# Twenty product units ahead of the chain, preparation without a floor, GpSimd for the first experts' split, and VectorE copies from step 13

## The chip, the cores and the metric

The kernel runs on one core of a Trainium2 chip. Its engines work in parallel and meet at semaphores: TensorE (PE in the rows) multiplies matrices, VectorE (DVE), ScalarE (ACT) and GpSimd (POOL) work element by element, and SyncE (SP), ScalarE and GpSimd issue DMAs. The metric is the time of one execution in device microseconds (us).

## The reference, cut to what matters

Three stages follow one another. The first is a delta rule over 768 time steps with a 48 x 48 state for each of 32 heads; the second routes each of 3072 rows to the best of eight experts; the third is a dense layer on the rows that come out.

```python
for t in range(S):                                   # _attn_ref
    kt, vt, bt = (k_n[:, :, t], v[:, :, t], beta[:, :, t, None])
    y[:, :, t] = np.einsum('bhd,bhde->bhe', q[:, :, t], state)
    v_old = np.einsum('bhde,bhd->bhe', state, kt)
    state = state + bt[:, :, :, None] * np.einsum('bhd,bhe->bhde', kt, vt - v_old)
...
e_idx = np.argmax(x @ w_gate, axis=1)                # _moe_ref: x is y, 3072 rows of 384
h = np.maximum(x[mask] @ w1[e], 0.0)                 # for each expert e
out[mask] = gate_w[mask, None] * eom[mask, e, None] * (h @ w2[e])
...
h = np.maximum(np.maximum(x @ w1, x @ w2), x @ w3)   # _moe2_ref
return h @ w_out
```

## The kernel before

The 768 time steps are cut into 24 chunks of 32. Within a chunk the recurrence is a triangular system, so the kernel inverts one 32 x 32 triangle for each chunk, batch and head, and then needs only matrix products from chunk to chunk. This second part is the **chain**: 24 steps, each of which needs the state that the step before it left.

**Product units.** `prods(p, j)` (L150 to L178) makes the products of keys with keys and keys with queries for the two chunks of pair p and one half j of the heads: 32 matmuls (64 rows in the profile) on TensorE, two copies on ScalarE, a mask on GpSimd (L147). There are 24 such units. After the second half of a pair ScalarE issues the store of the products (`gd`, from slice 2 on, L174) and the loads of the two `KQT` chunks (112 x 1024 values of 4 bytes, 448 KB each) that lie two pairs ahead. `NA` says how many units stand in front of the chain; the rest are put at 0.05, 0.50, 0.95, ... of the chain's steps.

**Inversion.** Four chunks make a slice, six slices in all. VectorE inverts a slice in 30 small steps (L239 and L245, both operands in on-chip memory). Before it comes the preparation: `inv_load` reads the stored products back (`Z<-gd`, SyncE), `inv_n1` takes the diagonal and the triangle on GpSimd (`vss`, L195; affine select, L196), `inv_n2` makes scales on ScalarE (`vn`, L202) and `inv_n3` finishes them on VectorE and GpSimd (L216 to L225, with the scaling of Z, L218). A planner in `run` spreads the inversion's steps over the chain by a budget of VectorE time in each step (`BUD`, `take`) and puts the four preparations `prep` = 2.8, 2.2, 1.5 and 0.6 steps ahead of the slice's start.

**A step of the chain.** `c_ks` multiplies by the state (`pR`, L318) and VectorE subtracts (`R`, L321); `c_u` multiplies by the inverted triangle (`pU`, L340), whose two halves go out in four copies each (`Ubd`, L348 on ScalarE or L350 on VectorE); `c_s` updates the state (`pS`, L360), again copied in two halves (`Sbd`, L367 or L369); `c_y` makes the output rows. Up to step `END` - 1 ScalarE makes all copies, from `END` on VectorE makes the second halves. SyncE loads the step's `kv` (L294) and inverted triangles (`TT`, L302), and GpSimd scales half of `kv` (`vscale`, L308), two steps ahead of the use. `R` of step i needs the scaled `kv` of step i.

**The experts' start.** From step 7 on routed rows are scattered into a table (`tab`, L474, GpSimd). From step 15 the weights of the first two experts are loaded (`r`, L679, SyncE) and split into a high and a low part (`w_0h` by a cast, L695; `w_0l` by a subtraction, L696): three pieces of 1024 columns from step 18.2, four of 768 from 19.3, three of 1024 from 23.0. The raw tile of the second group is the one into which the third group is loaded. At steps 21 to 23 the first rows are gathered (`xg`, L837) and turned (`pt`, L852). After the chain come ten runs of expert work and six blocks of the dense layer, TensorE-bound for the most part.

Program order sets each engine's order: the lists in `run` are written out engine by engine as they stand, and an engine takes its instructions strictly one after the other.

Of the kernel before, what the change touches and what calls it, by code (L numbers as in the profile page):

```python
# [22 lines left out]
def merge(*lists):  # L23

    items = []
    for li, l in enumerate(lists):
        n = len(l)
        for j, f in enumerate(l):
            items.append(((j + 0.5) / n, li, j, f))
    items.sort(key=lambda t: t[:3])  # L30
    return [t[3] for t in items]


class Attn:
# [9 lines left out]
    def __init__(s, ctx, tc, psum, big, hp, gp, kqt, knv, bt, wgt, xd, tab, ctab, cum, ident, wrm, x2):  # L44
        s.tc, s.nc, s.psum, s.big, s.hp, s.gp = tc, tc.nc, psum, big, hp, gp
        nc = tc.nc
        s.kqt, s.knv, s.btd, s.wgtd, s.xd, s.tab, s.ctab, s.cum = kqt, knv, bt, wgt, xd, tab, ctab, cum
        s.ident, s.wrm, s.ones, s.x2 = ident, wrm, wrm[:, 0:128], x2
        s.NI = 24
        s.NP = 12  # L50
        s.NSL = 6
        s.RLB = "m"
        s.XB, s.xTs, s.RLK = 1, {}, 0
        s.CUT = 0.95
        s.NL = 4
        s.NA = 14
        s.LATE = 0.4
        s.W = (0, 1, 0)
        s.END = 16
        s.TU, s.TB, s.MF = (22.92, 22.95, 22.97), "TRT", 2  # L60

        s.BUD = (5.0, 5.6, 4.6, 5.0)

        s.ORD = {0: 0, 1: 14, 2: 36, 3: 50, 4: 66, 5: 80}
        s.prep = (2.8, 2.2, 1.5, 0.6)
        cp = s.cp = ctx.enter_context(tc.tile_pool(name="acst", bufs=1))
        s.p2 = ctx.enter_context(tc.tile_pool(name="ap2", bufs=2))
        s.dr = ctx.enter_context(tc.tile_pool(name="adr", bufs=1, space=DRAM))
        nc.scalar.preload_act_table_set("natural_log_exp_and_others")
        s.chain = False  # L70
        s.RT, s.RD, s.LT = (15.4, (15.9, 0.3), (17.4, 0.35), (20.7, 0.25)), 0.5, ((18.2, 0.45), (19.3, 0.35), (23.0, 0.05))
        s.KQT, s.AT, s.Gd, s.kv, s.TT, s.x, s.inv = {}, {}, {}, {}, {}, {}, {}
# [415 lines left out]
    def run(s, pre, tail):  # L488
        nc, NI, NP = s.nc, s.NI, s.NP
        for i in range(s.NL):  # L490
            s.loadKQ(i)
        s.consts()
        s.warm(9)
        A = [lambda p=p, j=j: s.prods(p, j) for p in range(NP) for j in range(2)]
        for k in range(4):
            A[k]()
        s.inv_load(0)
        for f in (s.inv_n1, s.inv_n2, s.inv_n3):
            f(0)
        B = [u[2] for u in s.steps(s.ORD)[:30]]  # L500
        s1 = s.ORD[1]
        for f in merge(B[:s1 // 3], [A[4], A[5]]) + merge(B[s1 // 3:s1 // 2], [A[6], A[7]]):
            f()
        s.inv_load(1)
        for f in (s.inv_n1, s.inv_n2, s.inv_n3):
            f(1)
        for f in merge(B[s1 // 2:], [A[8], lambda: s.load32(0), A[9], s.empty, A[10], lambda: s.load32(1), A[11], lambda: s.inv_load(2), A[12], A[13]]):
            f()
        s.inv_end(0)
        s.warm(8, s.inv[0]["tt"])  # L510
        s.inv_store(0)
        s.vscale(0)
        s.vscale(1)

        spr = [[] for _ in range(NI + 1)]
        put = lambda t, f: spr[int(t + 1)].append(((t + 1) % 1, f))
        t, left = [-1.0], [s.BUD[0]]
        s.ends = []

        def take(c):  # L520
            while left[0] < c:
                t[0] = int(t[0]) + 1.0 if t[0] >= 0 else 0.0
                left[0] += s.bud(int(t[0]))
            left[0] -= c
            b = s.BUD[0] if t[0] < 0 else s.bud(int(t[0]))
            t[0] = (int(t[0]) if t[0] >= 0 else -1) + min(0.99, max(0, 1 - (left[0] + c) / b))
        for starts in (s.ORD,):
            for st, c, f, en in s.steps(starts)[30:]:
                take(c)
                put(t[0], f)  # L530
                for sl in st:
                    t0 = t[0]
                    for dt, g in zip(s.prep, (s.inv_load, s.inv_n1, s.inv_n2, s.inv_n3)):
                        if sl > 2:
                            put(max(0.6, t0 - dt), lambda g=g, sl=sl: g(sl))
                        elif sl == 2 and g != s.inv_load:
                            put(-1 + (t0 + 1) * (0.3, 0.5, 0.9)[(s.inv_n1, s.inv_n2, s.inv_n3).index(g)], lambda g=g: g(2))
                    s.ends.append(("start", sl, t0))
                for sl in en:
                    take(1.4)  # L540
                    put(t[0], lambda sl=sl: s.inv_end(sl))
                    assert t[0] + s.LATE < 4 * sl - 1, (sl, t[0])
                    put(t[0] + s.LATE, lambda sl=sl: s.inv_store(sl))
                    s.ends.append((sl, t[0]))
        for k, f in enumerate(A[s.NA:]):
            put(0.05 + k * 0.45, f)
        for t, f in pre(s):
            put(t, f)
        s.chain = True
        for i in range(-1, NI):  # L550
            sp = [f for _, f in sorted(spr[i + 1], key=lambda x: x[0])]
            if i < 0:
                for f in sp:
                    f()
                continue
            q, k = i // 4 - 1, i % 4
            x0 = [lambda: s.r_g(q)] if q >= 0 and k == 1 else [lambda: s.r_p(q)] if q >= 0 and k == 2 else []
            f1 = [lambda: (s.x_store(i - 1), s.r_t(i - 1))] if i else []
            f2 = [lambda: s.r_l(q)] if q >= 0 and k == 0 else []
            s.load32(i + 2)  # L560
            if i >= 7:
                s.r_s({19: [0, 1], 20: [2, 3], 21: [], 22: [], 23: [0, 1]}.get(i, [(i - 7) % 4]))
            n = round(len(sp) * s.CUT) if i < 20 else sum(t < s.CUT for t, _ in spr[i + 1])
            wm = lambda k: [lambda: s.warm(s.W[k])]
            fl = [lambda: s.c_ks(i), lambda: s.c_qs(i)] + x0 + wm(0) + merge([lambda: s.c_u(i)] + f1, sp[:n]) + wm(1)
            fl += [lambda: s.c_s(i)] + merge([lambda: s.c_y(i)] + f2, sp[n:]) + wm(2)
            fl += [lambda: s.loadT(i + 2), lambda: s.vscale(i + 2)]
            for f in fl:
                f()
        tail(s)  # L570


class Decode:
# [17 lines left out]
    def units(s, raw, w):  # L591

        nc, V, N = s.nc, s.nc.vector, s.N
        n, a = s.pieces.pop(0)
# [30 lines left out]
class Moe:  # L625
# [394 lines left out]

    def ahead(s, a):

        V = s.nc.vector
        v = {}

        def later(key, n, t, d):
            def go(j):
                if (key, n) not in v:
                    v[key, n] = s.split(key, n, V, V)
                v[key, n][j]()  # L1030
            return [(t + d * j, lambda j=j: go(j)) for j in range((3, 4)[n])]

        def lists():
            s.ids(0)
            s.ids(1)

        def rows(k):
            for c in range(2):
                s.gather(k, c)

        def turned():
            z = [a.p2.tile([128, 1024], F32R, tag="Z", name=f"xT0{j}", bufs=4) for j in range(2)]
            s.xT[0] = [tuple(z[c // 2][:, (c % 2 * 2 + j) * 256:(c % 2 * 2 + j) * 256 + 256] for j in range(2)) for c in range(3)]

        def turn(c):
            if c == 0:
                turned()
            s.xpose(0, c, a.TB[c])
        def raws(key, n, slot, t, d):
            us = s.raws(key, n, lambda: s.btile(slot, f"r{n}_{key}", F32), 3)  # L1050
            return [(t + d * j, u) for j, u in enumerate(us)]
        out = [(a.RT[0], s.first), (a.RT[0] + a.RD, s.first_values), (19.3, s.parts), (21.0, lists),
               (21.3, lambda: rows(0)), (21.6, lambda: rows(1))]
        for (key, n, slot), (t, d) in zip(((0, 0, 0), (0, 1, 1), (1, 0, 1)), a.RT[1:]):
            out += raws(key, n, slot, t, d)
        for (key, n), (t, d) in zip(((0, 0), (0, 1), (1, 0)), a.LT):
            out += later(key, n, t, d)
        out += [(t, lambda c=c: turn(c)) for c, t in enumerate(a.TU)]
        out += [(23.1 + 0.1 * f, lambda f=f: s.m1(0, f)) for f in range(a.MF)]
        return out  # L1060
# [201 lines left out]
```

## Time and profile before

| what | value |
|---|---|
| median of 3 runs | 861.08 us (859.71 to 863.37) |
| the profiled execution's own time | 862.21 us |
| span of its instructions | 860.5 us |
| TensorE busy | 745.3 us (87%) |
| VectorE busy | 487.8 us (57%) |
| ScalarE busy | 303.9 us (35%) |
| GpSimd busy | 247.8 us (29%) |

The table counts the whole execution. The change touches the first 340 us or so; there the engines' shares differ from those of the whole, which is why the rows below are taken stretch by stretch. A row of the timeline gives start, duration, engine, line, operation, what is written and read, the count of merged instructions, and in brackets the engine's idle time before and what ended it.

### The profile page before, as it was taken

How to read it: one execution, taken by the hardware profiler on the slowest of the kernel's cores; microseconds unless marked ns; L12 is line 12 of the kernel's file. 1: busy time of each engine (PE TensorE's matmuls, PEld its weight loads, DVE VectorE, ACT ScalarE, POOL GpSimd, SP SyncE). 2: the span in 40 equal slices, each digit the busy share in tenths (PEclk: the TensorE clock that was granted, in tenths of full speed). 3: DMA queues.
4: the chain of work that ended last, by engine and by line, in shares of the span. 5: the costliest groups of instructions: out<-in, count | busy, mean ns of one | idle time of the engine just before them, and what ended most of it. 6: DMA issues, size and time to landing. Idle time of an engine off the chain costs nothing.

```text
span 860.5 us, 20328 instructions
## 1 busy us (share of the span) xinstructions
PE 745.3 (87%) x8516; PEld 631.0 (73%) x8517; DVE 487.8 (57%) x1142; ACT 303.9 (35%) x693; POOL 247.8 (29%) x326
## 2 busy tenths in 40 slices
PE   7615777788677987999989999999999999999997
PEld 5504555455455886989888889889888898988886
DVE  3896668994575753788899997132231323223130
ACT  2203556777433332454444353122121222212121
POOL 5715446732333232166455322000001010100101
PEclk9997879999978998999999999999999999999999
DMA  8743755444926226667786783921002020000001
GB/s 225 172 133 100 182 117 151 110 122 128 251 55 171 74 60 189 217 214 230 260 259 227 242 301 131 384 82 48 26 1 74 1 73 2 19 19 1 37 1 40
DMA packets 85756, 110.28 MB, mean 128 GB/s; under 512 B 53860, under 2 KB 67115, under 8 KB 82971
## 3 DMA queue, kind: packets, MB, share of 16 engines
q1 hardware_dynamic: 57259, 87.08, 32.4%
q10 hardware_dynamic: 19360, 11.42, 5.5%
q0 software_dynamic: 9040, 10.42, 4.1%
q8 instruction: 69, 1.13, 0.6%
q14 instruction: 28, 0.23, 0.1%
HBM read 79.53 MB, written 29.36 MB: 127 GB/s over the span
## 4 chain that ended last, share of the span: by engine, by line
PE 45%; DVE 11%; DMA 7%; issue 3%; SPq 1%; ACT 1%; POOL 1%; POOLq 0%; DVEq 0%; ACTq 0%
PE pm L864 26%; PE pz L864 8%; PE po L864 6%; PE ph L864 3%; DMA wd<-work 3%; DMA wm<-wd 2%; DVE hl L889 1%; DVE work L609 1%; SPq L821 1%; DVE work L611 1%; DMA work<-in_ma_dram 1%; DVE work L607 1%; DVE work L608 1%; DVE work L612 1%; DMA TT<-td 1%
## 5 line engine op out<-in xcount | busy, mean ns | idle before, releaser
L864 PE MATMUL pm<-xhm,wm 128*128 128x512 f32 x648 | 204.8, 396 | 1.9 <-DMA wm<-wd 1.9
L937 DVE TENSOR_TENSOR work<-work,pm 128x512 f32<-128x512 f32 x72 | 49.5, 688 | 186.8 <-PE pm L864 186.8
L864 PEld LDWEIGHTS pm<-xhm,wm 128*128 128x128 f32 x648 | 121.8, 188 | 31.2 <-DMA wm<-wd 2.3
L864 PE MATMUL pm<-xlm,wm 128*128 128x512 f32 x324 | 128.2, 396 | 0.0
L950 POOL DMA_INDIRECT out_dram<-work,idm x24 | 23.7, 986 | 303.7 <-ACT work L949 289.2
L939 ACT CAST hmh<-work 128x512 fp32r<-128x512 f32 x36 | 22.4, 622 | 156.3 <-DVE work L937 156.3
L864 PE MATMUL pz<-wm,hmh 128*128 128x384 f32 x320 | 73.7, 334 | 0.0
L239 DVE TENSOR_TENSOR zt<-Z 128x30 f32<-128x30 f32 (+14 forms) x219 | 71.5, 365 | 3.2 <-POOL Z L218 2.6
L864 PEld LDWEIGHTS pm<-xlm,wm 128*128 128x128 f32 x324 | 61.0, 188 | 14.4
L348 ACT COPY Ubd<-pU 32x192 f32<-32x192 f32 x160 | 49.5, 309 | 52.6 <-PE pU L340 49.7
L245 DVE TENSOR_TENSOR Z<-Z,zt 128x30 f32<-128x30 f32 (+14 forms) x219 | 61.0, 318 | 0.0
L864 PEld LDWEIGHTS pz<-wm,hmh 128*128 128x128 f32 x320 | 57.2, 188 | 0.5
L360 PE MATMUL pS<-Ubd,kv 128*48 128x192 f32 x368 | 44.4, 377 | 14.7 <-ACT Ubd L348 10.9
L837 POOL DMA_INDIRECT xg<-xd,ids x32 | 44.6, 1393 | 41.4 <-PE pt L852 29.2
L164 PE MATMUL pg<-KQT 48*32 48x64 f32 x1536 | 38.1, 279 | 16.6 <-DMA KQT<-in_kqt_dram 9.8
L360 PEld LDWEIGHTS pS<-Ubd,kv 128*48 128x48 f32 x368 | 23.7, 138 | 38.7 <-ACT Ubd L348 20.6
L164 PEld LDWEIGHTS pg<-KQT 48*32 48x32 f32 x1536 | 32.5, 143 | 23.4 <-issue 15.9
L367 ACT COPY Sbd<-pS 48x384 f32<-48x384 f32 x78 | 36.8, 472 | 14.1 <-PE pS L360 12.9
L899 ACT COPY y<-po 128x256 f32<-128x256 f32 (+6 forms) x30 | 13.3, 444 | 78.4 <-PE po L864 78.4
L318 PE MATMUL pR<-Sbd,KQT 112*32 112x96 f32 x736 | 23.9, 256 | 18.1 <-ACT Sbd L367 13.8
L308 POOL TENSOR_TENSOR kv<-kv,TT 128x384 f32<-128x384 f32 x20 | 21.0, 1050 | 64.2 <-DMA TT<-td 32.4
L864 PE MATMUL pz<-wm,hml 128*128 128x384 f32 x112 | 37.4, 334 | 0.0
(303 smaller groups left out, 1648.9 us busy)
## 6 DMA issues: line engine op xcount, KB each, us to landing
raw<-in_w_dram SPq DMA_DIRECT2D x13, 1536.0 KB
kv<-in_knv_dram SPq DMA_DIRECT2D x24, 384.0 KB
wd<-work SPq DMA_DIRECT2D x24, 384.0 KB
wm<-wd SPq DMA_DIRECT2D x8, 1152.0 KB
KQT<-in_kqt_dram ACTq DMA_DIRECT2D x20, 448.0 KB
xd<-x SPq DMA_DIRECT2D x24, 192.0 KB
r<-in_w_dram SPq DMA_DIRECT2D x9, 512.0 KB
raw<-x SPq DMA_DIRECT2D x6, 768.0 KB
```

What stands on the lines that cost most here:

```text
L164: nc.tensor.matmul(ps[b * 32:b * 32 + 32, o:o + 64], kq[:, 0, :], kq.rearrange("p k t -> p (k t)"), start=True, stop=True, tile_position=( ...
L239: nc.vector.tensor_mul(t, Z[:, a:e, m].unsqueeze(2).to_broadcast([128, e - a, n]), Z[:, m, m + 1:].unsqueeze(1).to_broadcast([128, e - a, n]))
L245: nc.vector.tensor_add(Z[:, a:e, m + 1:], Z[:, a:e, m + 1:], t)
L318: nc.tensor.matmul(ps[b * 32:b * 32 + 32, g * 96:g * 96 + 96], s.KQT[i][:, b, g, 0, :], s.Sbd[0:112, b, g, :], start=True, stop=True, tile ...
L348: nc.scalar.copy(dst, src)
L360: nc.tensor.matmul(s.pS[q][j * 64:j * 64 + 48, g2 * 192:g2 * 192 + 192], s.kv[i][:, 0, h, :], s.Ubd[h // 4][:, h % 4, :], start=(i == 0 an ...
L367: nc.scalar.copy(dst, src)
L837: s.nc.gpsimd.indirect_dma_start(t[0:r.ct], None, s.xd[0:2049] if k < 2 else s.xd, bass.IndirectOffsetOnAxis(s.gid[k][0:r.ct, c, 0:1], 0))
L864: s.nc.tensor.matmul(ps, a, b, start=(start and k == 0), stop=(stop and k == n - 1))
L937: nc.vector.tensor_max(m, m, ps)
L939: nc.scalar.copy(hi, m)
L950: nc.gpsimd.indirect_dma_start(s.out, bass.IndirectOffsetOnAxis(i[:, c, 2:3], 0), y, None, bounds_check=3071, oob_is_err=False)
```

## The change

`NA` goes from 14 to 20: six more product units stand ahead of the chain, and the last four take the first places in it. The lower limit of 0.6 steps falls away for the preparation of slices 3 to 5. `END` goes from 16 to 13, so steps 13 to 15 have their second copies on VectorE. The split of the first two experts' weights is given to GpSimd, both the cast and the subtraction.

```diff
-        s.NA = 14
+        s.NA = 20
...
-        s.END = 16
+        s.END = 13
...
-        for f in merge(B[s1 // 2:], [A[8], lambda: s.load32(0), A[9], s.empty, A[10], lambda: s.load32(1), A[11], lambda: s.inv_load(2), A[12], A[13]]):
+        for f in merge(B[s1 // 2:], [A[8], lambda: s.load32(0), A[9], s.empty, A[10], lambda: s.load32(1), A[11], lambda: s.inv_load(2)] + A[12:s.NA]):
...
-                            put(max(0.6, t0 - dt), lambda g=g, sl=sl: g(sl))
+                            put(t0 - dt, lambda g=g, sl=sl: g(sl))
...
-        V = s.nc.vector
+        G = s.nc.gpsimd
...
-                    v[key, n] = s.split(key, n, V, V)
+                    v[key, n] = s.split(key, n, G, G)
```

On TensorE in step 2 of the chain, before: `pU` is that step's product, `pg` are product units (pair and half), `pX` turns the step's output rows, `pwarm` is a dummy product, `pS` the update of the state.

```order
L340 MATMUL pU0_2_1596<-R2_1565,T0_998 32x48 x16
L340 MATMUL pU1_2_1597<-R2_1565,T0_998 32x48 x16
L164 MATMUL pg9_1_1644<-KQT18_1209 32x64 x32
L391 MATMUL pX1_1698<-ident_80,x1_1506 128x128 x3
L164 MATMUL pg10_0_1705<-KQT18_1209 32x64 x16
L164 MATMUL pg10_0_1705<-KQT21_1436 32x64 x16
L485 LDWEIGHTS wrm_58
L485 MATMUL pwarm_1755<-wrm_58 128x512
L360 MATMUL pS0_160<-Ubd0_156,kv2_1061 48x192 x4
```

The same place now:

```order
L340 MATMUL pU0_2_1784<-R2_1753,T0_1229 32x48 x16
L340 MATMUL pU1_2_1785<-R2_1753,T0_1229 32x48 x16
L391 MATMUL pX1_1847<-ident_80,x1_1731 128x128 x3
L485 LDWEIGHTS wrm_58
L485 MATMUL pwarm_1866<-wrm_58 128x512
L360 MATMUL pS0_160<-Ubd0_156,kv2_1302 48x192 x4
```

No product unit stands between `pU` and `pS` of step 2 any more. From `R` of step 2 to `R` of step 5 there were five units and are none; from step 1 to step 2 there were two and is one; in step 0 there are three as before.

On SyncE ahead of the chain and in its first steps, before: `Z2` and `Z3` are the products of slices 2 and 3 read back, `kv` the chunks' keys and values.

```order
L294 DMA kv1_801<-in_knv_dram 128x768
L184 DMA Z2_867<-gd2_164 128x1024
L294 DMA kv2_1061<-in_knv_dram 128x768
L184 DMA Z3_1213<-gd3_165 128x1024
L294 DMA kv3_1303<-in_knv_dram 128x768
```

And now:

```order
L294 DMA kv1_771<-in_knv_dram 128x768
L184 DMA Z2_831<-gd2_164 128x1024
L184 DMA Z3_1253<-gd3_165 128x1024
L294 DMA kv2_1302<-in_knv_dram 128x768
L294 DMA kv3_1531<-in_knv_dram 128x768
```

The load of slice 3 has moved ahead of `kv2`. VectorE's order in these steps has not changed by a row; on GpSimd two masks that stood ahead of slice 3's `vss` now stand behind it, and six masks stand ahead of the first scaling of `kv`.

On GpSimd in steps 18 to 21, before: `kv` rows are the scaling, `tab` the scatter, `rohb` and `cum` the count of rows, `xg` the gather.

```order
L460 COPY rdat3_4290<-tok_194 128x4
L308 TENSOR_TENSOR kv20_4240<-kv20_4240,TT20_4380 128x384
L474 DMA tab_78<-rdat3_4290,rpos3_4299 25600x3 x2
L308 TENSOR_TENSOR kv21_4383<-kv21_4383,TT21_4509 128x384
L474 DMA tab_78<-rdat3_4290,rpos3_4299 25600x3 x2
L308 TENSOR_TENSOR kv22_4512<-kv22_4512,TT22_4646 128x384
L433 TENSOR_TENSOR cum_74<-cum_74,rohb4_4701 128x8 x4
```

The later part of the same stretch now:

```order
L308 TENSOR_TENSOR kv21_4383<-kv21_4383,TT21_4509 128x384
L474 DMA tab_78<-rdat3_4290,rpos3_4299 25600x3 x2
L695 CAST w1_0h_4473<-r1_0_4203 128x768
L696 TENSOR_TENSOR w1_0l_4474<-r1_0_4203,w1_0h_4473 128x768
L695 CAST w1_0h_4473<-r1_0_4203 128x768
L696 TENSOR_TENSOR w1_0l_4474<-r1_0_4203,w1_0h_4473 128x768
L308 TENSOR_TENSOR kv22_4512<-kv22_4512,TT22_4646 128x384
L433 TENSOR_TENSOR cum_74<-cum_74,rohb4_4701 128x8 x4
```

Two pieces of the second group stand between the last scatter and `kv22`; two more and a piece of the first group stand ahead of `kv21`, and two pieces of the first group ahead of `kv20`. The third group stands in step 23 between the second and the third scatter of the rows of steps 16 to 19 (`rdat4`).

## Rows read from the trace of the kernel before

**Rows 1.** Stretches: start:end, length, each engine's busy time and count, clock, DMA share, GB/s.
```profile
44.00:54.00 10.00, 0.00 (x0) 0.00 (x0) 10.00 (x39) 0.00 (x0) 0.51 (x1) 1.00 0.90 246
54.00:62.00 8.00, 0.17 (x1) 0.20 (x2) 7.97 (x31) 0.00 (x0) 0.11 (x1) 1.00 0.00 0
94.94:132.23 37.29, 30.21 (x852) 21.25 (x848) 20.27 (x73) 20.18 (x58) 17.94 (x21) 0.77 0.57 142
132.23:194.44 62.21, 48.26 (x1377) 32.38 (x1369) 58.47 (x224) 43.22 (x121) 33.66 (x42) 1.00 0.50 129
```
**Rows 2.** Timeline of VectorE: the subtraction R of steps 1, 2, 5, 13.
```profile
83.12 0.55 DVE L321 TENSOR_TENSOR R<-kv,pR 128x384 f32<-128x384 f32 x1 [4.10 <-PE pR L318]
94.94 0.55 DVE L321 TENSOR_TENSOR R<-kv,pR 128x384 f32<-128x384 f32 x1 [1.32 <-POOL vn L225]
...
132.23 0.56 DVE L321 TENSOR_TENSOR R<-kv,pR 128x384 f32<-128x384 f32 x1 [4.01 <-POOL vn L224]
...
194.44 0.55 DVE L321 TENSOR_TENSOR R<-kv,pR 128x384 f32<-128x384 f32 x1
```
**Rows 3.** Timeline of step 2: ScalarE and TensorE.
```profile
98.69 1.27 ACT L348 COPY Ubd<-pU 32x192 f32<-32x192 f32 x4 [1.24 <-PE pU L340]
...
103.62 2.80 PE L360 MATMUL pS<-Ubd,kv 128*48 128x192 f32 x16
```
**Rows 4.** Timeline from the chain's start to R of step 1.
```profile
64.08 1.53 DVE L245 TENSOR_TENSOR Z<-Z,zt 128x126 f32<-128x126 f32 x2
...
75.35 1.45 POOL L147 TENSOR_TENSOR AT<-AT,maskA 128x256 f32<-128x256 f32 x2
...
76.14 0.99 DVE L239 TENSOR_TENSOR zt<-Z 128x108 f32<-128x108 f32 x2
77.05 0.46 DVE L245 TENSOR_TENSOR Z<-Z,zt 128x108 f32<-128x108 f32 x2
...
79.35 0.32 POOL L195 TENSOR_SCALAR vss<-Z 128x32 f32<-128x32 f32 x1 [2.55 <-DMA Z<-gd]
...
80.21 1.92 ACT L367 COPY Sbd<-pS 48x384 f32<-48x384 f32 x4
```
**Rows 5.** Timeline of VectorE: R of steps 16 and 17.
```profile
216.28 0.56 DVE L321 TENSOR_TENSOR R<-kv,pR 128x384 f32<-128x384 f32 x1 [4.52 <-PE pR L318]
222.69 0.55 DVE L321 TENSOR_TENSOR R<-kv,pR 128x384 f32<-128x384 f32 x1 [0.99 <-issue]
```
**Rows 6.** Waits of SyncE's queue from 200 to 300: total us, times, longest.
```profile
SPq L679 <- DVE w_0l L696: 10.2, 1, 10.2
```
**Rows 7.** Timeline of SyncE in step 20: the next expert's load.
```profile
259.43 0.35 SPq L679 DMA_DIRECT2D r<-in_w_dram  x1
```
**Rows 8.** Timeline of GpSimd from step 18 to the chain's end.
```profile
233.80 0.19 POOL L460 COPY rdat<-tok 128x4 int32<-128x4 int32 x1
...
267.68 0.84 POOL L308 TENSOR_TENSOR kv<-kv,TT 128x384 f32<-128x384 f32 x1 [13.57 <-DVE Sbd L369]
...
275.88 1.03 POOL L474 DMA_INDIRECT tab<-rdat,rpos  x1 [0.28 <-POOL rdat L460]
278.91 0.97 POOL L474 DMA_INDIRECT tab<-rdat,rpos  x1 [2.00 <-DMA tab<-rdat,rpos]
...
294.53 1.02 POOL L433 TENSOR_TENSOR cum<-cum,rohb 128x8 bf16<-128x8 bf16 x4 [6.96 <-DVE rog L435]
```
**Rows 9.** Timeline of step 21: VectorE, R of step 22.
```profile
268.55 0.55 DVE L321 TENSOR_TENSOR R<-kv,pR 128x384 f32<-128x384 f32 x1 [1.11 <-POOL kv L308]
```
**Rows 10.** GpSimd's groups by form: busy, mean ns of one, idle before.
```profile
L218 POOL TENSOR_TENSOR Z<-Z,vnw 128x1024 f32<-128x1024 f32 x5 | 12.3, 2452 | 0.4
...
L196 POOL TENSOR_SCALAR_AFFINE_SELECT Z<-Z 128x1024 f32<-128x1024 f32 x6 | 7.7, 1283 | 1.6 <-DVE vss L195 1.2
```
**Rows 11.** Source line 696: duration ns min/median/max, first and last start us.
```profile
L696 POOL TENSOR_TENSOR w_2l<-raw,w_2h x4: 1831/1880/2819, 362.8 to 378.8; 128x768 fp32r<-128x768 f32 x4
```
**Rows 12.** Costliest groups: the product units' matmuls, 64 rows to a unit.
```profile
L164 PE MATMUL pg<-KQT 48*32 48x64 f32 x1536 | 38.1, 279 | 16.6 <-DMA KQT<-in_kqt_dram 9.8
```

## The prediction
> **What bounds the kernel now.** I read the time of the chain's steps first, then what ends the wait in front of each, then the durations. All the edits lie in the first 340 us or so; the experts and the dense layer behind them have the same work in the same order, so I count a microsecond gained or lost at the chain's end as one of the total.
>
> The step is measured from one subtraction R to the next. Step 1 takes 11.82 us, steps 2 to 4 together 37.29, that is 12.43 each, and steps 5 to 12 together 62.21, that is 7.78 each [rows 2]. The stretches say what stands behind the two speeds [rows 1]: in steps 5 to 12 VectorE is busy 58.47 of 62.21 us, so the inversion sets the pace. In steps 2 to 4 it is busy 20.27 of 37.29, 6.76 per step; no engine that computes is full except TensorE with 30.21, and that at a granted clock of 0.77. Step 2 shows how: the last four `Ubd` copies, which the state's update needs, end at 99.96, and the update `pS` starts at 103.62 [rows 3]. What stands between in TensorE's order are two product units, and the second of them needs a buffer that ScalarE frees only behind the copies, a store and two loads. So TensorE's order, not TensorE's work, is what holds steps 2 to 4.
>
> Ahead of the chain it is VectorE alone: from 44 to 54 it is busy all of the time, and from 54 to 62 for 7.97 of 8.00 us, with TensorE, ScalarE and the DMAs idle [rows 1].
>
> From step 18 on a queue holds the chain. SyncE waited 10.2 us for VectorE's last split of the second group [rows 6], since the third group's load goes into that raw tile; the load goes out at 259.43 [rows 7], the inverted triangles of chunk 22 are queued behind it, GpSimd scales `kv` 22 at 267.68 to 268.52 after 13.57 us of idling [rows 8], and R of step 22 starts at 268.55 with that as its releaser [rows 9]. Nothing of slack is left in this line.
>
> **Steps 0 to 4: the units.** Six units leave the steps: one from step 1, five from steps 2 to 4, while step 0 keeps three. Without units, steps 2 to 4 are steps like 5 to 12. I take 7.78 each, 23.3 for the three, a gain of 14.0. The bounds: steps 13 to 15, where the inversion ends, take 21.84 in all or 7.28 each [rows 2, 5], which would make it 15.4; if only TensorE's own time of the units came out, it would be 5 units of 64 rows at 38.1/1536 us [rows 12], 1.59 each, 8.0 in all. Step 1 is full on VectorE save for the 1.32 us in front of R of step 2 [rows 2]; I take a gain of 1.0 (0 to 1.3).
>
> **Step 0: three things that cancel.** Now R of step 1 comes after 4.10 us of idling [rows 2]: ScalarE is blocked by the scales of slice 3, whose `vss` on GpSimd starts at 79.35 after waiting 2.55 us for the products to be read back, and the state's copies stand behind them, at 80.21 [rows 4]. With the load ahead of `kv2` this wait goes, and the two masks (1.45 us) now stand behind `vss`. What is late next is VectorE itself. Two-operand steps stand still beside a GpSimd operation: two of them beside two masks took 0.99 us where the next two took 0.46, so 0.53 for a mask [rows 4]. The six masks that move ahead of the chain now fall into the stretch that VectorE fills, with no GpSimd work there before [rows 1]: 6 x 0.53 = 3.2 us later for everything. And slice 3's affine select, 1.28 us [rows 10], which ran in the idle time, comes to lie beside the inversion; two steps beside such a one took 1.53 [rows 4]. Sum: -4.1 + 3.2 + 1.3 = +0.4. Bounds: -4.1 without any collision, and +5 if the loads come late (a rival below). VectorE's order is as before, so the planner's edit gives no more than this.
>
> The loads have room: three `gd` stores, six `KQT` loads and one reading back (0.8, 2.8 and 0.5 MB by the shapes) at the 246 GB/s of the stretch before take 16.5 us from about 54, 8 of which were empty [rows 1]. What the units ahead of the chain need of that (a store, two loads, the reading back, 1.7 MB) is there by 61; the rest is needed in steps 0 and 1.
>
> **Steps 13 to 15: second copies.** These steps take 7.28 on average [rows 2, 5]; step 16, which has its second copies on VectorE, takes 6.41 [rows 5]. Twice 0.87, and a quarter in step 13, where VectorE still has the last slice in front of them: a gain of 2.0 (0 to 2.6).
>
> **Steps 18 to 22: the split on GpSimd.** GpSimd comes to the first piece at 233.99 [rows 8]. Until the tile is free it then has seven pieces, two scalings and two pairs of scatters. A subtraction of 768 columns takes it 1.88 us [rows 11], one of 1024 is priced by the product of that size, 2.45 [rows 10]: 3 x 2.45 + 4 x 1.88 = 14.9. A large cast on GpSimd is in no row. The nearest is the affine select, one operand in and one out, 1.28 for 1024 columns [rows 10], so 0.96 for 768: 3 x 1.28 + 4 x 0.96 = 7.7. From below the fixed cost of a small operation, 0.32 [rows 4], would make 2.2; from above the two-operand price would make 14.9. I take 7.7. The scalings are 0.84 each, the scatters run from 275.88 to 279.88 for a pair, 4.0 [rows 8]: 1.7 + 8.0. Sum: 233.99 + 14.9 + 7.7 + 1.7 + 8.0 = 266.3 against 259.43. As shown, what is behind this load has no slack: R of step 22 comes 6.8 later (1.4 to 14.0), and what VectorE gains in steps 19 and 20 by being rid of the split is waited away there.
>
> The Trainium skill ("GPSIMD Engine Reference", section 4.1 Engine selection) warns against two-operand work on this engine, which our 1.88 us bears out, but says one-operand work goes at roughly line rate; by the 1.03 cycles per element of its section 3.1 a cast of 1024 would be, as an estimate, 0.88 us, and the total 2.4 lower.
>
> TensorE idles those 6.8 us more ahead of step 22, and would start it at the lower clock, as at `pS` of step 2, which took 2.80 [rows 3]; no row prices this, and I set 1.0 (0 to 3).
>
> **Step 23.** The third group, 3 x 3.73 = 11.2 us, stands between the second scatter's end, 279.88, and two more scatters: 279.88 + 11.2 + 4.0 = 295.1 against the count at 294.53 [rows 8], both before the common shift. So 0.6 late, up to 4 with the dear cast. The cover is the 6.96 us that GpSimd waits there for VectorE.
>
> **Sum.** +0.4 - 1.0 - 14.0 - 2.0 + 6.8 + 1.0 + 0.6 = -8.2 us on the profiled execution's 862.21, so 854.0. The median of the runs is 1.1 under that execution; I predict 853.
>
> **Rivals.**
> 1. *GpSimd becomes the bound from step 18 on, and the kernel is slower.* If casts cost what subtractions cost and the subtractions run at the slow end of their row, 2.82 for 768 [rows 11] and 3.76 for 1024, the seven pieces take 37.3 instead of 22.6, the load goes out 14.7 later still, and the third group's 18.6 us push the count back by 7.4 more: 875 at worst. With every second subtraction at the slow end (5.8 less) it is 869, the figure I give it. Speaking for it: a strict queue, and a reader without slack. Against: the subtraction's median is 1.88. From 16.6 us lost in steps 18 to 23 on (14.0 + 1.0 + 2.0 - 0.4) it eats all that the rest gains. Chance 0.09.
> 2. *Only the cast is dear*, at 2.45 and 1.84: 7.2 more at the load and 3.5 in step 23, 864. Chance 0.10.
> 3. *The units were not what made steps 2 to 4 long*, and only their 8.0 us of TensorE come out: 6 more, 859. For it: TensorE's low clock there and idle time that the profile gives no reason for. With the clock at 0.77 in these steps as now, their TensorE work of 6.03 us per step (48.26/8) would grow by 1.8, 858, so I put both together. Chance 0.11. The Trainium skill speaks for the clock's part ("TensorE: Matmul & The Clock Gate", What's actually happening): the slow clock is the default and activity lifts it, and the units are activity. Against it: steps 5 to 12 have no units and were granted 1.00 throughout [rows 1].
> 4. *The chain starts late*: units 18 and 19 wait for their loads, their masks stand on GpSimd ahead of the scaling of `kv` 0. 5 us, 858. Chance 0.08.
> 5. *Better than the forecast*: full chain pace at 7.28 and cheaper casts, step 0 gaining some: 846. Chance 0.12.
>
> **How the numbers follow.** The forecast has 0.50, with a range of its own of 849 to 857. Taking in rival 5 on one side and the dear cast on the other gives 843 to 864. A measurement of this kernel tells some 0.5% from no change, 4.3 us: faster means under 856.8, slower over 865.4. Faster: most of the forecast, 0.47, rival 5, 0.12, and 0.07 of rivals 3 and 4, in all 0.66. Slower: rival 1, 0.09. The rest, 0.25, is within.
>
> **What the profile of the changed kernel would show.** R of step 1 near 83.5; R of step 5 near 117.6 instead of 132.23, with steps 2 to 4 under 8.5 us, VectorE over 85% busy in them and the clock at 1.00. From 44 to 62 six masks on GpSimd and VectorE's steps beside them at twice their time. Steps 14 and 15 near 6.4. A cast of 1024 on GpSimd near 1.3 us, SyncE waiting for GpSimd's subtraction instead of VectorE's, and the third group's load going out some 32 us after that copy of `rdat` on GpSimd, where it was 25.4 (259.43 - 233.99). The forecast is wrong if steps 2 to 4 stay over 10 us, if R of step 22 is not released by the scaling of `kv`, or if the cast is off 1.3 by a factor of two.

## The result, and the profile of the changed kernel

The changed kernel took 853.45 us (median of 11 runs, 849.14 to 857.62) against 863.37 us for the kernel before on the same chip (11 runs, 858.7 to 867.55): a ratio of 0.9894 with a 95% interval of 0.9868 to 0.992. Forecast was 853 in a range of 843 to 864, from a median of 861.08. The profiled execution took 854.27 us with a span of 852.6.

The stretches of [rows 1], in the same columns, with the last two moved to where the steps now lie (steps 2 to 4, steps 5 to 12):

```profile
44.00:54.00 10.00, 4.32 (x164) 3.69 (x159) 9.97 (x41) 1.20 (x4) 4.68 (x1) 0.50 0.88 225
54.00:62.00 8.00, 5.96 (x224) 5.03 (x216) 8.00 (x22) 2.26 (x8) 7.40 (x5) 0.50 0.94 220
94.83:119.86 25.03, 19.23 (x546) 13.62 (x541) 23.13 (x72) 16.30 (x46) 9.25 (x14) 0.93 0.50 143
119.86:183.00 63.14, 48.01 (x1341) 32.97 (x1349) 59.22 (x225) 43.21 (x121) 35.19 (x46) 0.97 0.49 118
```

Steps 2 to 4 take 25.03 us where they took 37.29, and VectorE is busy for 92% of them (23.13 of 25.03): they have become steps like 5 to 12. Ahead of the chain VectorE has no idle time, as before, but GpSimd, TensorE and the DMAs now work beside it. R (L321) on VectorE's timeline, to be held against [rows 2, 5, 9]; the bracket is the idle time before it and its releaser:

```profile
84.52 0.54 DVE L321 TENSOR_TENSOR R<-kv,pR 128x384 f32<-128x384 f32 x1
94.83 0.55 DVE L321 TENSOR_TENSOR R<-kv,pR 128x384 f32<-128x384 f32 x1 [0.79 <-POOL vr L223]
...
119.86 0.54 DVE L321 TENSOR_TENSOR R<-kv,pR 128x384 f32<-128x384 f32 x1
...
183.00 0.55 DVE L321 TENSOR_TENSOR R<-kv,pR 128x384 f32<-128x384 f32 x1
...
248.13 0.56 DVE L321 TENSOR_TENSOR R<-kv,pR 128x384 f32<-128x384 f32 x1 [4.43 <-POOL kv L308]
264.87 0.56 DVE L321 TENSOR_TENSOR R<-kv,pR 128x384 f32<-128x384 f32 x1 [9.46 <-POOL kv L308]
277.56 0.55 DVE L321 TENSOR_TENSOR R<-kv,pR 128x384 f32<-128x384 f32 x1
```

The 4.10 us of idling in front of R of step 1 [rows 2] are gone, and still it is 1.4 us later than in the trace of before; R of step 5 is 12.4 earlier, and up to step 19 it stays 11 to 12.4 ahead. R of step 22 is only 3.7 earlier: step 21 alone takes 16.74 us, 9.46 of it VectorE's wait for the scaling of `kv`. The split's place in this is in GpSimd's timeline (each piece is a cast L695 and a subtraction L696) and in SyncE's waits and issues:

```profile
225.07 1.01 POOL L474 DMA_INDIRECT tab<-rdat,rpos  x1 [3.72 <-DMA tab<-rdat,rpos]
...
226.22 0.19 POOL L460 COPY rdat<-tok 128x4 int32<-128x4 int32 x1
226.34 1.03 POOL L695 CAST w_0h<-r 128x1024 fp32r<-128x1024 f32 x1
227.46 2.35 POOL L696 TENSOR_TENSOR w_0l<-r,w_0h 128x1024 fp32r<-128x1024 f32 x1
...
254.39 0.82 POOL L695 CAST w_0h<-r 128x768 fp32r<-128x768 f32 x1
255.29 1.81 POOL L696 TENSOR_TENSOR w_0l<-r,w_0h 128x768 fp32r<-128x768 f32 x1
264.00 0.84 POOL L308 TENSOR_TENSOR kv<-kv,TT 128x384 f32<-128x384 f32 x1 [6.90 <-DMA TT<-td]
```
```profile
SPq L679 <- POOL w_0l L696: 20.0, 1, 20.0
```
```profile
257.13 0.35 SPq L679 DMA_DIRECT2D r<-in_w_dram  x1
257.52 0.42 SPq L384 DMA_DIRECT2D xd<-x  x1
258.14 0.34 SPq L679 DMA_DIRECT2D r<-in_w_dram  x1
258.53 0.47 SPq L302 DMA_DIRECT2D TT<-td  x1
```

SyncE now waits 20.0 us for GpSimd's last subtraction (10.2 for VectorE's in [rows 6]). The third group's load goes out at 257.13, 30.9 us after the start of that copy of `rdat` (25.6 before, from 233.80 to 259.43); `TT` of chunk 22 goes out behind it at 258.53, and GpSimd, idle by then, waits 6.90 us for it.

### The profile page after: what moved, and what is told of

Read it like the earlier page. It is cut to its first block, busy times and chain, and to the rows that moved or that the text cites. A ratio compares the mean times of both kernels' runs of the same rounds, so it can differ in the third digit from the quotient of the medians.

```text
span 852.6 us, 20332 instructions
## 1 busy us (share of the span) xinstructions
PE 746.0 (87%) x8506; PEld 635.6 (75%) x8517; DVE 479.7 (56%) x1140; ACT 297.8 (35%) x675; POOL 279.3 (33%) x346
## 3 DMA queue, kind: packets, MB, share of 16 engines
q0 software_dynamic: 9040, 10.42, 4.1%
## 5 line engine op out<-in xcount | busy, mean ns | idle before, releaser
L239 DVE TENSOR_TENSOR zt<-Z 128x30 f32<-128x30 f32 (+14 forms) x219 | 74.3, 378 | 3.2 <-POOL Z L218 2.6
L348 ACT COPY Ubd<-pU 32x192 f32<-32x192 f32 x148 | 45.8, 309 | 66.4 <-PE pU L340 63.5
L245 DVE TENSOR_TENSOR Z<-Z,zt 128x30 f32<-128x30 f32 (+14 forms) x219 | 66.2, 342 | 0.0
L164 PE MATMUL pg<-KQT 48*32 48x64 f32 x1536 | 40.3, 293 | 21.6 <-DMA KQT<-in_kqt_dram 17.6
L164 PEld LDWEIGHTS pg<-KQT 48*32 48x32 f32 x1536 | 34.5, 152 | 28.5 <-issue 15.8
L367 ACT COPY Sbd<-pS 48x384 f32<-48x384 f32 x72 | 34.0, 472 | 14.2 <-PE pS L360 13.1
L888 ACT ACTIVATE hh<-ph 128x440 fp32r<-128x440 f32 (+5 forms) x48 | 24.0, 502 | 33.9 <-PE ph L864 33.6
```

Source lines behind the costliest of these rows:

```text
L164: nc.tensor.matmul(ps[b * 32:b * 32 + 32, o:o + 64], kq[:, 0, :], kq.rearrange("p k t -> p (k t)"), start=True, stop=True, tile_position=( ...
L239: nc.vector.tensor_mul(t, Z[:, a:e, m].unsqueeze(2).to_broadcast([128, e - a, n]), Z[:, m, m + 1:].unsqueeze(1).to_broadcast([128, e - a, n]))
L245: nc.vector.tensor_add(Z[:, a:e, m + 1:], Z[:, a:e, m + 1:], t)
L348: nc.scalar.copy(dst, src)
L367: nc.scalar.copy(dst, src)
L888: nc.scalar.activation(hi, ps, AF.Relu)
```

## Experiments

All places in us from the span's start, each from one trace; the ratio is to the kernel before on the same chip, with its interval. "13-15" is R of step 13 to R of step 16, "18-22" R of step 18 to R of step 23, "tail" R of step 23 to the end, where all kernels have the same work (the third group's split, at its start, on the engine that the kernel gives it).

```
kernel                     R1      R5   13-15  18-22   tail   ratio
before                   83.12  132.23  21.84  50.38  578.3
b_slot5                  84.39  134.20  21.71  49.52  576.6  .9955 [.9922,.9989]
a_na14                   84.61  135.00  20.94  58.05  578.3  1.0097 [1.0066,1.0129]
b_units                  84.60  119.02  21.57  49.44  575.0  .9817 [.9778,.9855]
changed                  84.52  119.86  20.93  57.77  575.0  .9894 [.9868,.992]
changed, second trace    84.74  118.02  20.76  58.20  573.2  .9894 [.9859,.993]
a_vv                     84.90  119.32  20.53  48.68  572.8  .9829 [.9789,.9868]
a_end16                  84.78  119.26  21.43  55.30  574.8  .9909 [.9877,.9941]
a_masks                  81.14  116.00  21.71  58.44  574.1  .9907 [.9873,.9942]
a_slot5                  85.78  120.23  21.62  48.81  577.2  .984 [.9789,.9891]
a_slot5_vv               84.83  119.28  20.95  46.32  574.4  .9774 [.9734,.9815]
a_slot5_vv_masks         81.77  116.24  22.73  46.65  576.7  .9728 [.9687,.9769]
a_gv                     80.76  115.12  22.48  47.55  574.9  .9777 [.9742,.9813]
a_gv_lt                  81.61  115.89  22.44  43.63  575.3  .9842 [.9801,.9883]
```

**The split alone (a_vv).**
```
-        G = s.nc.gpsimd
+        V = s.nc.vector
-                    v[key, n] = s.split(key, n, G, G)
+                    v[key, n] = s.split(key, n, V, V)
```


> The changed kernel with the three early splits back on VectorE (casts and subtractions), all else as changed. Theory G (the split on GpSimd delays the load that goes into the second group's raw tile, and this delay is lost at the end): the third group's load goes out near 247.4 (259.43 of the kernel before, less the 12.0 us by which steps 16 to 18 come earlier) instead of 257.1, step 21 falls from 16.7 us to under 9, R of step 22 comes near 256.5 instead of 264.9, and the time is 845 to 848. Rival F (what the freed VectorE gives back in steps 19 and 20 and behind the chain is worth as much): R of step 22 comes at most 3 us earlier than in the changed kernel, or the gain is gone by the first expert run, and the time is 851 to 856.

844.34 us (before: 860.76). The load went out at 245.53, R of step 22 stood at 254.24:

```profile
254.24 0.56 DVE L321 TENSOR_TENSOR R<-kv,pR 128x384 f32<-128x384 f32 x1 [0.72 <-POOL cum L433]
```
```profile
SPq L679 <- DVE w_0l L696: 6.8, 1, 6.8
```

Theory G holds: with VectorE splitting, step 21 takes 6.87 us, steps 18 to 22 take 48.68 instead of 57.77, and `kv` no longer releases R. The split on GpSimd is a loss within a change that gains. (The run moves all three early groups, so the third group's part in step 23 is in this price.)

**The units undone (a_na14), and the units alone (b_units).**
```
a_na14:   -        s.NA = 20                        +        s.NA = 14
          -  put(t0 - dt, lambda ...)               +  put(max(0.6, t0 - dt), lambda ...)
b_units:  the kernel before with the opposite of these two edits
```


> The changed kernel with 14 units ahead of the chain again and the planner's lower bound of 0.6 put back; second copies and split as changed. Theory U (the units in steps 2 to 4 cost what the two traces show, 12.3 us in these steps, less the 3.2 us that the six masks cost ahead of the chain): the second slice-0 transpose n0 is back at 61.6, R of step 5 stands near 132, steps 2 to 4 take 12 to 13 us each, and the time is 862 to 866. Rival (the gate of step 22 waits for something that doesn't move with the chain, so that part of the 12 us is lost there anyway): R of step 5 near 132, but R of step 22 less than 8 us later than in the changed kernel, and the time is 855 to 860.

> The kernel before with one part of the change alone: twenty units ahead of the chain, and the scales without the lower bound of 0.6. Theory: the three parts add up as -14 (units; R of step 5 stood at 132.2, 135.0 and 134.2 in three traces with fourteen units ahead and at 119.3 to 120.2 in the six with twenty whose masks were not moved), 0 (second copies) and +7 (split): R of step 5 at 119 to 120, and the time 14 us under that of the kernel before, with the copies worth nothing the same as with the splits on VectorE alone (844.3). Rival: the units and the second copies only work together (VectorE, freed of units, could take the copies), and the time is 848 to 852.

a_na14 took 870.78 us, more than theory U allowed, and b_units 845.53 (before: 861.34), 15.8 less than the kernel before; a_vv, which has the second copies too, has the same ratio. So the units carry the gain, the second copies add nothing to be measured, and their rivals fall. Both runs move the planner's bound together with the units; no run parts the two. R of step 5 stands at 132.23, 135.00 and 134.20 in the three traces with fourteen units ahead, and between 118.02 and 120.23 in the seven with twenty and their masks in place: 133.8 against 119.3 in the mean. The profile of before had the shortest steps 2 to 4 of the three (37.29 us; 38.20 and 38.06 in the others).

**The second copies undone (a_end16).**
```
-        s.END = 13
+        s.END = 16
```


> The changed kernel with the second half of the copies on ScalarE until step 16 again. As predicted for the change, steps 13 to 15 would be 2.0 us longer together and the time 855.5. By the two traces (steps 14 and 15 gained 0.9 and 0.4, steps 13 and 16 lost 0.5 each) there is nothing in it: R of step 17 within 0.7 us of the changed kernel's, the time 853 to 854.

851.35 us, a ratio of 0.9909 against 0.9894: no difference to be measured, as the two traces said, though times with these intervals couldn't tell 2.0 us from nothing. R of step 17 stands 0.7 earlier than in the first trace of the changed kernel and 2.2 later than in its second.

**The masks moved (a_masks).**
```
-        s.mask(p, j)
+        if not 7 <= p < 10:
+            s.mask(p, j)
...
+        for p in range(7, 10):
+            for j in range(2):
+                put(6.1 + p + 0.4 * j, lambda p=p, j=j: s.mask(p, j))
```


> The changed kernel with the six masks of units 14 to 19 (pairs 7 to 9) taken from the stretch ahead of the chain and put into steps 13 to 15, where the inversion is over. Theory C (a two-operand step of VectorE stands still beside a mask on GpSimd): n0 comes back from 64.8 to 61.6, R of steps 1 to 13 are 3.2 us earlier, and the time is 850 to 851. Rival (the stretch ahead of the chain is longer for the more transfers, ScalarE copies or products): n0 stays within 0.7 us of 64.8 and the time is 853 to 854. If the masks, 6 x 1.45 us, are late for the products that read them in steps 14 to 18, these steps grow and the gain is given back there.

`n0`, VectorE's transpose that ends its work ahead of the chain and that the first scaling of `kv` waits for, came back from 64.83 to 61.45, R of step 1 to 81.14. VectorE's steps, in the changed kernel beside masks and in this one without them, and GpSimd's masks in the changed kernel (five of the six merged into the first row) show why:

```profile
57.49 1.08 DVE L239 TENSOR_TENSOR zt<-Z 128x84 f32<-128x84 f32 x2
58.50 1.62 DVE L245 TENSOR_TENSOR Z<-Z,zt 128x84 f32<-128x84 f32 x2
60.04 1.62 DVE L239 TENSOR_TENSOR zt<-Z 128x58 f32<-128x58 f32 x2
61.59 0.53 DVE L245 TENSOR_TENSOR Z<-Z,zt 128x58 f32<-128x58 f32 x2
```
```profile
49.31 12.08 POOL L147 TENSOR_TENSOR AT<-AT,maskA 128x256 f32<-128x256 f32 x5 [5.69 <-ACT AT L170]
62.41 0.72 POOL L147 TENSOR_TENSOR AT<-AT,maskA 128x256 f32<-128x256 f32 x1 [1.01 <-ACT AT L170]
```
```profile
57.31 0.55 DVE L240 TENSOR_TENSOR zt<-Z 128x84 f32<-128x84 f32 x2
57.79 0.55 DVE L246 TENSOR_TENSOR Z<-Z,zt 128x84 f32<-128x84 f32 x2
58.26 0.53 DVE L240 TENSOR_TENSOR zt<-Z 128x58 f32<-128x58 f32 x2
58.71 0.53 DVE L246 TENSOR_TENSOR Z<-Z,zt 128x58 f32<-128x58 f32 x2
```

Theory C holds for the place. In the time nothing of it shows: 851.5 us beside a_end16's 851.35 on the same chip, and a ratio of 0.9907 where the changed kernel has 0.9894. Step 20 took 12.40 us, 9.76 and 9.30 in the two traces of the changed kernel, so most of what the chain had won was waited for there. How much of it is left at the chain's end the traces don't settle: R of step 23 stands at 273.95, at 277.56 and 275.13 in the changed kernel and at 273.99 in a_end16.

**Another tile for the third group (a_slot5, b_slot5, a_slot5_vv), and the masks moved as well (a_slot5_vv_masks).**
```
-    SLOT = (((2, 3), (5, 6)), ((4, 0), (7, 1)))
+    SLOT = (((2, 3), (6, 1)), ((4, 0), (7, 5)))
-        ... zip(((0, 0, 0), (0, 1, 1), (1, 0, 1)), a.RT[1:]):
+        ... zip(((0, 0, 0), (0, 1, 1), (1, 0, 5)), a.RT[1:]):
```


> The changed kernel, the split still on GpSimd, with the third group's raw tile in the fifth large tile (free since step 17) in place of the second group's, so that its load, and the chunk's loads queued behind it on SyncE, wait for no split. Theory Q (SyncE's queue is what carries GpSimd's delay to the chain): the wait of 20.0 us on SyncE is gone, the three loads go out before 240, the scaling of kv 22 comes right behind the last piece, near 258 instead of 264.0, R of step 22 near 259 and the time 846 to 849. Rival P (GpSimd's own queue does it: the seven pieces stand ahead of the scaling of kv 22 whatever SyncE does): the scaling of kv 22 not before 262, the time 852 to 855.

> The kernel before with the same other tile for the third group. By the prediction's reading nothing has slack behind this load: the wait of 10.2 us on SyncE is gone, R of step 22 is not released by the scaling of kv any more, the gathers of the first rows come earlier, steps 22 and 21 shrink by 5 us together, and the time is 855 to 857. Rival: step 21 was 7.3 us long with the wait, as long as it is without, so only the gathers in step 22 come earlier, and what they save is under 2 us: 858 to 861.

> The changed kernel with the splits on VectorE and the other tile for the third group. Theory Q: the wait of 6.8 us that SyncE still had with the splits on VectorE is gone, the lists and rows of the first expert come earlier, TensorE's 3.3 us of waiting for these rows in step 22 go, and the time is 839 to 842 (844.3 with the splits on VectorE alone). Rival: these rows wait for the scatters and not for SyncE; step 22 stays at 13 us and the time is 844 to 846.

> The same with the six masks moved to steps 13 to 15. In the kernel with the masks moved alone, R of step 1 to 20 came 3.4 to 6.3 us earlier, but R of step 21 as with nothing moved, since GpSimd's pieces of the split took the gain. If that is so, it must come through here, where GpSimd has no pieces: R of step 23 3 us earlier than in the kernel with the other tile and VectorE's split, and the time 836 to 839. Rival: the masks are in the way in steps 13 to 18 themselves, and the time is that of the same kernel without them moved, within 1 us.

a_slot5 took 848.61 us (before: 862.2); its loads went out at 239.75, 241.06 and 252.24, `kv` 22 was scaled at 254.76 (rival P: not before 262), and with all seven pieces still on GpSimd steps 18 to 22 took 48.81 us, as with the splits on VectorE and the old tile. So in the traces it is SyncE's queue that carries most of GpSimd's delay to the chain: theory Q, though R of step 22, at 262.57, came 3.6 later than it said. GpSimd's own queue is not free either. VectorE and GpSimd in step 21 of a_slot5:

```profile
249.49 0.78 DVE L423 TENSOR_TENSOR rd<-rl,rm 128x32 f32<-128x32 f32 x1
250.31 1.84 DVE L425 SCALAR_TENSOR_TENSOR rsel<-rd,wts 128x32 f32<-128x32 f32 x1
252.19 0.19 DVE L427 TENSOR_REDUCE rr<-rsel 128x4 f32<-128x32 f32 x1
252.41 0.51 DVE L429 TENSOR_TENSOR roh<-wts,rr 128x32 f32<-128x32 f32 x1
...
253.04 1.80 DVE L435 TENSOR_TENSOR rog<-roh,rl 128x32 f32<-128x32 f32 x1
...
254.98 1.45 DVE L350 COPY Ubd<-pU 32x192 f32<-32x192 f32 x4
```
```profile
249.38 0.84 POOL L695 CAST w_0h<-r 128x768 fp32r<-128x768 f32 x1
250.31 1.80 POOL L696 TENSOR_TENSOR w_0l<-r,w_0h 128x768 fp32r<-128x768 f32 x1
...
252.95 1.84 POOL L696 TENSOR_TENSOR w_0l<-r,w_0h 128x768 fp32r<-128x768 f32 x1
254.76 0.84 POOL L308 TENSOR_TENSOR kv<-kv,TT 128x384 f32<-128x384 f32 x1
```

Two small routing steps, 0.19 us elsewhere, last as long as the subtractions beside them, and the copies of `Ubd` stand behind. In b_slot5 the 10.2 us wait of [rows 6] is gone too, but it took 860.06 us, 2.1 less than before, and steps 18 to 22 only 0.9: the rival was right. In the kernel before something else stands close behind that load, so that bringing it forward gains little; what a later load costs this run doesn't show.

a_slot5_vv took 843.64 and a_slot5_vv_masks 840.66 us, both beside a_slot5 on one chip. The first lies between what theory Q (839 to 842) and its rival (844 to 846) expected: step 22 did fall, from 13.28 to 7.80 us, but step 21 grew from 6.87 to 9.67. It also gives the fair price of the split with this tile: steps 18 to 22 take 46.32 us with the splits on VectorE, 2.5 less than in a_slot5, and the time is 5.0 us less, as much as with the old tile (0.984 against 0.9774 here, 0.9894 against 0.9829 there). So the tile gains some 0.5% with the splits on either engine; that it takes away most of what GpSimd costs is seen in the traces of steps 18 to 22 and not in the times, whose intervals would also allow it. a_slot5_vv_masks shows the masks' gain coming through once GpSimd has no pieces: 3.0 us in time, R of step 23 2.6 earlier. It is the fastest version found, 0.9728 of before.

**Casts on GpSimd, subtractions on VectorE (a_gv; a_gv_lt with the pieces earlier and further apart); the changed kernel again (a_again).**
```
a_gv, from a_slot5_vv_masks:   +                    v[key, n] = s.split(key, n, G, V)
a_gv_lt, from a_gv:            LT's first pairs (18.2, 0.45), (19.3, 0.35) become (17.2, 0.6), (19.2, 0.6)
```


> The fastest kernel so far (splits on VectorE, the third group's other tile, masks in steps 13 to 15) with the split's casts on GpSimd and its subtractions on VectorE. Theory: GpSimd loses mostly by its subtractions (2.37 and 1.80 us, against 1.04 and 0.82 for a cast); seven casts are 6.4 us of its queue instead of 20.9 with the subtractions, and each piece takes 1.2 instead of 1.9 us from VectorE, which stood in front of the Sbd copies of steps 18 and 19: 2 to 4 us faster than VectorE alone, 837 to 839. Rival: any piece in GpSimd's queue holds up the scaling of kv behind it, and every subtraction now waits for GpSimd with VectorE's copies queued behind: slower than VectorE alone, 843 to 848.

> The same with the pieces of the two early groups 0.6 of a step apart from step 17.2 and 19.2 on, where they stood 0.45 and 0.35 apart from 18.2 and 19.3. If steps 18 and 19 are long because two pieces fall into one step and VectorE does them ahead of that step's Sbd copies, this is 2 us faster than the closer spacing: 835 to 837. Rival: the pieces come too early for their loads, wait on VectorE with the chain's copies behind them, and it is slower than the closer spacing by 2 us or more.

> The changed kernel once more, unaltered, for a second trace of it. Behind the chain its first trace took 575.0 us from R of step 23 to the end, the kernel before 578.3, with the same work. If these 3.3 us belong to the change, the second trace shows 575 again (574.5 to 575.5) and R of step 22 at 264.9. If it is the spread of the experts' phase (572.8 to 578.3 over ten traces of kernels that are alike there), it can be anywhere in it, and R of step 22, with GpSimd's pieces ahead of it, moves by some us as well (260.2 in the trace with the copies of steps 13 to 15 on ScalarE).

a_gv took 841.82 us, between what its two sides expected; its ratio can't be told from that of a_slot5_vv_masks. VectorE's subtraction of 1024 columns, 1.22 us in a_vv, took 2.83 and 3.39 there, as GpSimd's next casts and a scaling of `kv` run beside it, one cast the first time and two the second (the first row holds two subtractions, of 2.83 and 1.21):

```profile
221.65 3.97 DVE L700 TENSOR_TENSOR w_0l<-r,w_0h 128x1024 fp32r<-128x1024 f32 x2 [2.31 <-POOL w_0h L699]
...
229.56 3.39 DVE L700 TENSOR_TENSOR w_0l<-r,w_0h 128x1024 fp32r<-128x1024 f32 x1 [1.26 <-POOL w_0h L699]
```

In a_gv_lt the rival came true, 846.99 us: the first subtraction stood 6.48 us on VectorE with the copies of step 17 behind it, which took 17.6 us:

```profile
216.79 2.02 DVE L700 TENSOR_TENSOR w_0l<-r,w_0h 128x1024 fp32r<-128x1024 f32 x1 [6.48 <-POOL w_0h L699]
218.74 1.45 DVE L351 COPY Ubd<-pU 32x192 f32<-32x192 f32 x4
```

The second trace of the changed kernel has R of step 22 at 261.78 (264.87 in the first) and a tail of 573.2 us: neither is a fixed number of this kernel.

## Why the prediction was right

**Steps 0 to 4: right.** -14.6 predicted (+0.4, -1.0 and -14.0), -14.5 measured as the means of R of step 5. Within it, in means of the same traces, step 0 came to +0.8 (R of step 1, 84.9 against 84.0), step 1 to -2.2 instead of -1.0, and steps 2 to 4 to -13.2: 8.2 us each and not 7.78. So the sum is closer than its parts, whose errors of 0.4, 1.2 and 0.8 cancel: that much is luck. Step 1 gained more than the bound of 1.3, which counted only VectorE's idle time; VectorE's busy time there fell as well, from 10.42 to 9.45 us in the two profiles, beside less work on GpSimd (7.07 and 5.08 us). The collision of six masks with VectorE was priced at 3.2; the mean of `n0` moved by 3.0 with the units, and by 3.4 back when the masks went. Rival 3 falls, though a part of its sign came: the granted clock in steps 2 to 4 was 0.93, not 1.00, in the first trace (1.00 in the second). Rivals 4 and 5 fall too: the chain started 0.8 us late and not 5, and its pace was 8.2 us, not 7.28.

The Trainium skill ("SBUF — State Buffer", section SBUF: two separate sides) says that a GpSimd operation and a two-input one of VectorE hold their port pair in turn, each for its whole length. The trace of a_slot5 agrees: the two routing steps end 0.04 and 0.05 us behind the subtractions beside them.

**Steps 13 to 15: the step that failed.** The term was -2.0. In the four traces with the second copies on ScalarE and the masks in place steps 13 to 15 take 21.6 us, in the six with them on VectorE 21.0: 0.7 us in place of 2.0, and nothing of it to be seen in the time. Steps 14 and 15 do gain, 1.36 together in the mean where 1.74 was predicted. Step 13, from which I took a quarter of 0.87, grows by 0.67. VectorE in step 13 of the changed kernel:

```profile
186.09 1.50 DVE L350 COPY Ubd<-pU 32x192 f32<-32x192 f32 x4
187.62 0.20 DVE L252 COPY ttb<-vn 128x32 f32<-128x32 f32 x1
187.78 0.09 DVE L253 MEMSET Z<- 128x32 f32 x1
187.90 1.23 DVE L254 TENSOR_TENSOR ttb<-Z,vw 128x1024 f32<-128x1024 f32 x1
189.16 1.12 DVE L369 COPY Sbd<-pS 48x384 f32<-48x384 f32 x2
```

The last slice's end stands between its two kinds of copies, and TensorE waits for both (0.7 us each). I had named that slice, and still took a gain: the wait that it makes in step 13 is what the term left out.

**Steps 18 to 22: right in sum, in part by luck.** +6.8 and +1.0 predicted; steps 18 to 22 take 57.6 us in the mean of the five traces with the splits on GpSimd and the old tile and 49.1 in the two of twenty units with them on VectorE, +8.5 (+7.2 against the one trace of before). The load's delay against the copy of `rdat` was 5.3 instead of 6.8, mostly since a cast is cheaper than its nearest row: 1.03 to 1.05 us for 1024 columns and not 1.28. The estimate by the Trainium skill's "GPSIMD Engine Reference", section 3.1, was 0.88, so the trace lies between.

What made up for it was not in the sum: against R of step 18 the load is 9.7 us later (37.3, before 27.6), and 4.4 of that lie ahead of the first piece. The copy of `rdat` comes 6.4 us behind R of step 18 where it came 2.0 behind it, since the scatter in front of it waits 3.72 us for the scatter before. It comes more than 4 us behind R in six of the nine traces with `END` = 13 (a_gv_lt, with its pieces moved, left out) and in none of the four with `END` = 16; a_end16, where it comes 1.5 behind, has the shortest steps 18 to 22 of the five, 55.30 us. Whether the second copies do this stays open.

The cold TensorE was not to be seen as a term of its own: step 22 took 12.69 us, 13.64 before, and its `pS` 2.23 us, 2.80 before, so the kernel before already paid it. In time the split costs about 0.65% (0.9894 against 0.9829), some 5.6 us, and 8.4 by a_na14 (1.0097), which is the kernel before with the split and the second copies. Rivals 1 and 2, both with a dear cast, fall: in the changed kernel the subtractions ahead of the load took 2.35 to 2.37 and 1.80 to 1.83 us, not the slow end of their row.

**Step 23: nearly.** +0.6 predicted; the third group's last subtraction ended at 286.44 and the two scatters behind it started at 286.59 and 290.23. From R of step 23 to the count it takes 13.65 us where it took 12.34, +1.3.

**What was not in the sum.** From R of step 23 to the end the changed kernel took 575.0 and 573.2 us, before 578.3. Over the fourteen traces, of the same work, it is 572.8 to 578.3. The three with fourteen units have 576.6 to 578.3, but two with twenty (577.2, 576.7) lie among them, so whether the units have a part in these 2 to 3 us stays open. Without them the means of the chain's terms give -14.5 - 0.7 + 8.5 = -6.7 (step 23 belongs to the tail); measured were -9.1 (1.06% of 863), interval -11.4 to -6.9. So the predicted 853 owes some 2 us to something that the sum didn't hold, and its nearness to 853.45 is luck in two more ways: the forecast started from a median of 861.08, where the runs beside the changed kernel gave 863.37, and -8.2 was predicted where -9.1 was measured.

## What to carry to other kernels

When a slow engine is given work, follow the buffer it reads: here the next load into that buffer stood in the queue that feeds the chain, and another tile let that load go out 17 us earlier. In the traces this took back some 6 of the 8.5 us that the slower engine cost in these steps; the time still showed the full price, 5.0 us. So compare a repair with the version that doesn't need it. Work that is hidden on GpSimd is not free beside a full VectorE; moving six masks to where VectorE has room gave 3.4 us at the chain's start, but it reached the time only where no later gate took it. A single trace can sit 2 us to one side of those of kernels that are alike there, in the very stretch that carries the forecast.

## What the runs showed of the hardware

A cast from f32 to fp32r took GpSimd 1.03 to 1.05 us for 128x1024 and ScalarE 1.04, and the subtraction 2.35 on GpSimd and 1.22 on VectorE: for casts alone GpSimd is no slower than ScalarE. By the two widths (1.03 and 0.82 us for 1024 and 768 columns) I estimate 0.82 ns for a column and 0.19 us that don't depend on the width. One-operand work on GpSimd stops VectorE's two-operand work as well, as the prediction had read from the affine select (two steps in 1.53 us beside it [rows 4]): in a_slot5 a routing step of 0.19 us took 0.78 beside a cast of 0.84, and in a_gv the subtraction of 1.22 us took 2.83 beside a cast and a scaling of `kv`.
